# A forward Fourier step on 64x64 tiles of the matrix engine, and a reordered seam between two stages

## The chip, the cores and the metric

The kernel runs on one core of a Trainium2 chip. A core has a matrix engine (TensorE, PE in the profile; its weight loads are listed apart as PEld), a vector engine (VectorE, DVE), a scalar engine (ScalarE, ACT), GpSimd (POOL) and SyncE (SP), whose queue issues most of the transfers. Matmuls write to PSUM, eight banks of 128 partitions by 512 floats. The metric is device microseconds per execution. Before the change three runs took 1424.41, 1427.23 and 1429.85 us, so the median is 1427.23 us.

## The reference, cut to what matters

The input has 4096 positions with 640 columns, and everything is float32.

```
mod = silu(c) @ w_mod                          # six vectors of 640: sa, ca, ga, sb, cb, gb
h = layernorm(x) * (1 + ca) + sa
X = rfft2(h) over positions                    # 4096 real values -> 2049 frequencies
z = X split into 4 blocks of 160 columns       # complex block MLP, two layers, relu,
Y = softshrink(mlp2(relu(mlp1(z))), 0.01)      #   then soft shrink of real and imaginary part
x = x + ga * irfft2(Y)
h = layernorm(x) * (1 + cb) + sb
x = x + gb * ((silu(h @ w_gate) * (h @ w_up)) @ w_down)
```

## The kernel before, in words

The transform of 4096 points is split as 128 by 32. **Stage A** multiplies by a 128-point Fourier matrix and writes its result to memory (`s1`). **Stage B** does the 32-point transforms with their twiddle factors. The frequencies come in eight chunks `ch`, taken in the order `[3, 4, 5, 6, 0, 1, 2, 7]`; a chunk is one tile `g` of 128 partitions by 4 by 640, and a table `tb` with four 128x128 matrices. For each of five column tiles `t` of 128 columns (t = 4 holds the remainders of the four blocks) `stage_b(ch, t)` issues four f32 matmuls, one for each `j`: 128 columns of `g` are the weights, 128 columns of `tb` the moving side. The matrix `tb` couples only partitions with the same `p` (two groups), so half of each 128x128 matrix is zero. An f32 matmul appears in the trace as two weight loads and two matmuls, so one column tile is 8 matmuls there (line L631).

`evac_b` then scales the PSUM bank into `z`, a high part by ScalarE (L638) and a low part by VectorE (L639); for t = 4 it is `rem_high` and `rem_low` (L681, L685), and a round trip through memory. **The block MLP** follows: `stage_l1` (L727, 21 matmuls, PSUM tags p1 and p3), ScalarE and VectorE work on its result (L744 to L769), `stage_l2` (L795, 16 matmuls, tag p2), and the soft shrink on VectorE (`shrink_v`, L819 and L820). **The first inverse step** `stage_i` (L841) has 16 matmuls with 32 rows and 64 columns each, 32 in the trace, whose products go to four banks of the tags p2, p1, p1, p3; ScalarE copies them (L844), and they are written to memory (`s2`).

The whole frequency stage is one hand-written sequence of 32 steps `p = 4 * ch + b`: the layer-1 products of step p, one or two tiles of stage B for the next chunk, then now and then a small matmul `pm` that finishes one of the six vectors (`mod_sum`, L563 and L568), the inverse of an earlier half chunk in even steps, the shrink, and the layer-2 products of step p - 1. Each engine executes its instructions in the order written. Of the eight PSUM banks six belong to tags p1, p2 and p3, two banks each taken in turn; b0 and b1 are single banks: stage B uses b0 (b1 for t = 4), and `pm` uses b0 or b1 where a vector isn't put in p3.

**The seam.** Behind the last step the first four rows of the second half of the kernel are finished without a trip through memory: `first_c`, `first_z` and `first_e` (L1044, L1050, L1057) give them in PSUM as `py`, VectorE and GpSimd add them to `x` and normalise (L1066 to L1105), ScalarE makes the first normalised row (L1119), TensorE transposes rows 0 and 1, then rows 2 and 3 (L1918), and `first_g` takes them through the first gate matrix. In it `high` (L1924) and `whole` (L1932 on ScalarE, L1934 on VectorE) read the transposed rows, and `low` (L1938) makes the low parts for both halves of the rows. The last inverse, `stage_i(7, 1)`, stands behind the products of all four rows. From there on the feed-forward part runs under a planner with its own table of costs; its order is the same in both kernels.

Of the kernel before, what the change touches and what calls it, by code (L numbers as in the profile page):

```python
# [6 lines left out]
F32 = mybir.dt.float32  # L7
F32R = mybir.dt.float32r
# [5 lines left out]
P = 128  # L14
# [7 lines left out]
NCH = 8  # L22
# [4 lines left out]
CE = 4  # L27
LAM = 0.01
# [18 lines left out]
def constants():  # L47
# [38 lines left out]
    tb = tb.transpose(0, 3, 1, 2, 4, 5, 6).reshape(8, 4, 128, 128)[ORDER].reshape(32, 128, 128)  # L86
# [3 lines left out]
    tx = tx.transpose(2, 0, 1, 3).reshape(128, 2)  # L90
# [76 lines left out]
def body(tc, x, w1, b1, w2, b2, wg, wu, wd, c, wm, k_fa, k_tb, k_tx, k_bx, k_ga, k_ge, k_id, out, dbg=None):  # L167
# [4 lines left out]
    def f32(ap):  # L172
        return ap.bitcast(F32)
# [23 lines left out]
    with ExitStack() as top:  # L197
# [3 lines left out]

        def bank0(i, shape, name):
            return ps.tile(shape, F32, tag=f"b{i % 2}", bufs=1, name=name)
# [28 lines left out]
        with ExitStack() as af:  # L232
# [57 lines left out]
            def load_tb(ch):  # L290
                tb = lp.tile([P, 4, 128], F32, tag="tb", bufs=2, name=f"tb{ch}")
                nc.sync.dma_start(tb, k_tb[:, 4 * ch:4 * ch + 4])
                tbs[ch] = tb


            def load_g(ch, lo=0, hi=32, dma=None, cols=(slice(0, D),)):
# [6 lines left out]
                for e in cols:  # L303
                    (dma or nc.sync).dma_start(gs[ch][4 * lo:4 * hi, :, e], src[:, lo:hi, :, e].rearrange("q n j d -> n q j d"))
# [249 lines left out]
            def mod_sum(m, hf=0):  # L554
# [3 lines left out]
                elif m in (2, 5):  # L558
                    if m == 5:
                        gbb.append(low_p.tile([P, 320], F32, tag="m", bufs=4, name=f"gbb{hf}"))  # L560
                    pm = (bank0(1, [P, 512], f"pm{m}_{hf}") if hf else
                          ps.tile([P, 512], F32, tag="p3", name=f"pm{m}_{hf}"))
                    mm(pm[:, :320], ones, acc[:, 320 * hf:320 * hf + 320], start=True, stop=True)  # L563
                    act.activation(gab[:, 320 * hf:320 * hf + 320] if m == 2 else gbb[hf], pm[:, :320], AF.Copy)
                else:
                    pm = bank0(m, [P, 512], f"pm{m}")
# [55 lines left out]

            def stage_b(ch, t):
                g, tb = gs[ch], tbs[ch]
# [9 lines left out]
            def evac_b(ch, t):  # L634
                pb = pbs[ch, t]
                z = lp.tile([P, 2, 2, 258], F32R, tag="z", bufs=4, name=f"z{ch}_{t}")
                zs[ch, t] = z
                act.activation(z[:, 0, :, 0:256], pb, AF.Identity, scale=ca1[:, t:t + 1])  # L638
                dve.scalar_tensor_tensor(z[:, 1, :, 0:256], pb, ca1[:, t:t + 1],  # L639
                                         f32(z[:, 0, :, 0:256]), op0=OP.mult, op1=OP.subtract)  # L640
                if ch == CE:
                    pool.tensor_copy(z[:, 0, :, 0:257:256], f32(edge[:, 0, t]))
# [36 lines left out]
            def rem_high(ch):  # L679
                rt = rts[ch] = low_p.tile([P, 2, 2, 258], F32R, tag="wt", name=f"rt{ch}")  # L680
                act.activation(rt[:, 0, :, 0:256], pbs[ch, 4], AF.Identity, scale=ca1[:, 4:5])  # L681

            def rem_low(ch):
                rt = rts[ch]
                dve.scalar_tensor_tensor(rt[:, 1, :, 0:256], pbs[ch, 4], ca1[:, 4:5], f32(rt[:, 0, :, 0:256]),  # L685
                                         op0=OP.mult, op1=OP.subtract)
# [1902 lines left out]
```

## Time and profile before

| what | value |
|---|---|
| three runs, median | 1427.23 us |
| the profiled execution's own time | 1425.44 us |
| its span | 1423.7 us |
| TensorE busy | 1391.0 us, 98% |
| VectorE, ScalarE, GpSimd busy | 1096.3, 734.0, 536.0 us |
| steps p = 5 to 28 with stage B of chunks 2 to 7 | about 91 to 262 us of the span |
| seam | about 282 to 312 us |

Times in rows are microseconds from the start of the span. A row of the timeline has the start, the time until the last of the merged instructions ended, engine, line, operation, output<-inputs and a count; a square bracket at its end tells for how long the engine was idle before and what ended that. Matmuls are pipelined, so the time to the next matmul's start, not the duration, is what one costs. L12 is line 12 of the kernel that the row belongs to; the changed kernel's lines are about 60 higher (stage B 676, inverse 901, `pm` 580 and 585, `low` 2006).

### The profile page before, as it was taken

The numbers are of one execution on the slowest core, as the hardware profiler recorded it, in microseconds if no ns is written. First come the engines' busy times: TensorE is split into PE (matmuls) and PEld (weight loads), VectorE is DVE, ScalarE is ACT, GpSimd is POOL, SyncE is SP. The second block draws the span as 40 slices with busy tenths as digits, with TensorE's granted clock in tenths as the row PEclk, the third lists the DMA queues.
The fourth block names the chain that finished last, engine by engine and source line by source line (L and its number), as shares of the span: only waits on it lengthen the run. The fifth ranks groups of instructions, "written<-read, shape, count | busy, mean of one in ns | idle before, by whom it ended". The sixth has DMA issues, their size and how long they took to land.

```text
span 1423.7 us, 24436 instructions
## 1 busy us (share of the span) xinstructions
PE 1391.0 (98%) x8840; PEld 1308.9 (92%) x8840; DVE 1096.3 (77%) x1984; ACT 734.0 (52%) x1495; POOL 536.0 (38%) x632
## 2 busy tenths in 40 slices
PE   6899999989999999999999999999999999999999
PEld 2699999968889888999999999999999999999998
DVE  8888898798787888578878777888657668567765
ACT  7855555555444664455555456555444345245432
POOL 5300330135353544224334434433325454145532
PEclk9999999999999999999999999999999999999999
DMA  9866677567668989997877998778886667966552
GB/s 379 318 232 202 213 251 237 192 197 257 243 228 315 326 272 297 347 330 233 292 279 254 356 347 278 237 268 279 310 309 232 215 218 241 358 219 215 206 190 86
DMA packets 183179, 372.17 MB, mean 261 GB/s; under 512 B 21361, under 2 KB 104369, under 8 KB 181393
## 3 DMA queue, kind: packets, MB, share of 16 engines
q1 hardware_dynamic: 175200, 355.12, 72.1%
q0 software_dynamic: 6272, 12.85, 2.9%
q10 hardware_dynamic: 1584, 2.62, 0.5%
q8 instruction: 70, 1.15, 0.3%
q14 instruction: 53, 0.43, 0.1%
HBM read 265.68 MB, written 104.86 MB: 260 GB/s over the span
## 4 chain that ended last, share of the span: by engine, by line
PE 84%; DVE 8%; DMA 4%; ACT 1%; issue 1%; POOL 1%; SPq 0%; DVEq 0%; ACTq 0%; POOLq 0%
PE pd L2458 15%; PE pw L2139 8%; PE pw L2141 8%; PE pw L2140 8%; PE pc L795 5%; PE pd_X L2320 5%; PE pl L727 4%; PE pg L2004 4%; PE pg L2003 4%; PE pg L2005 4%; PE pd_Y L2320 3%; PE pw L2150 2%; PE pw L2152 2%; PE pw L2151 2%; PE pb L631 2%; PE py L1691 2%
## 5 line engine op out<-in xcount | busy, mean ns | idle before, releaser
L2458 PE MATMUL pd<-wdh,a 128*128 128x320 f32 x1040 | 239.1, 310 | 1.1 <-DVE x L2430 1.1
L2458 PEld LDWEIGHTS pd<-wdh,a 128*128 128x128 f32 x1040 | 176.2, 188 | 1.7 <-DVE x L2430 1.4
L2458 PE MATMUL pd<-wdl,a 128*128 128x320 f32 x540 | 166.2, 309 | 0.0
L1446 DVE TENSOR_TENSOR wb<-r,wb 128x512 fp32r<-128x512 f32 (+3 forms) x154 | 151.5, 994 | 12.0 <-ACT wb L1443 9.9
L2139 PE MATMUL pw<-h,wt 128*128 128x384 f32 x416 | 141.2, 340 | 2.2 <-ACT s_x L2158 2.2
L2141 PE MATMUL pw<-h,wt 128*128 128x384 f32 x416 | 140.2, 337 | 0.0
L2140 PE MATMUL pw<-h,wt 128*128 128x384 f32 x416 | 139.9, 336 | 0.0
L2430 DVE TENSOR_TENSOR x<-x,pd 128x320 f32<-128x320 f32 x240 | 109.7, 479 | 39.0 <-PE pd L2458 34.7
L1443 ACT ACTIVATE wb<-r 128x512 fp32r<-128x512 f32 (+3 forms) x170 | 117.4, 704 | 35.2 <-PE pw L2152 25.9
L2139 PE MATMUL pw<-h,wb 128*128 128x384 f32 x312 | 105.0, 336 | 0.9 <-DVE x L2430 0.9
L2140 PE MATMUL pw<-h,wb 128*128 128x384 f32 x312 | 104.6, 335 | 0.0
L2141 PE MATMUL pw<-h,wb 128*128 128x384 f32 x312 | 104.6, 335 | 0.0
L2003 PE MATMUL pg<-ht,wb 128*128 128x512 f32 x260 | 102.3, 393 | 0.0
L2005 PE MATMUL pg<-ht,wb 128*128 128x512 f32 x260 | 101.4, 390 | 0.3 <-DVE wb L1446 0.3
L2458 PEld LDWEIGHTS pd<-wdl,a 128*128 128x128 f32 x540 | 101.4, 188 | 0.3
L2004 PE MATMUL pg<-ht,wb 128*128 128x512 f32 x260 | 101.5, 390 | 0.0
L2158 ACT ACTIVATE s_x<-pw 128x384 f32<-128x384 f32 x52 | 25.4, 489 | 120.3 <-PE pw L2141 119.5
L1674 POOL TENSOR_TENSOR cr<-cr,gab 128x640 f32<-128x640 f32 x28 | 48.0, 1717 | 94.5 <-DMA cr<-s 67.1
L2139 PEld LDWEIGHTS pw<-h,wt 128*128 128x128 f32 x416 | 78.1, 188 | 3.7 <-ACT s_x L2158 3.7
L2140 PEld LDWEIGHTS pw<-h,wt 128*128 128x128 f32 x416 | 78.2, 188 | 0.0
L2141 PEld LDWEIGHTS pw<-h,wt 128*128 128x128 f32 x416 | 78.1, 188 | 0.0
L2294 DVE TENSOR_TENSOR x<-x,pd_X 128x320 f32<-128x320 f32 x144 | 64.5, 484 | 14.2 <-PE pd_X L2320 14.2
(344 smaller groups left out, 3879.8 us busy)
## 6 DMA issues: line engine op xcount, KB each, us to landing
wt<-td SPq DMA_DIRECT2D x104, 512.0 KB, 5.2
hs<-ho SPq DMA_DIRECT2D x52, 512.0 KB, 5.4
h<-hs SPq DMA_DIRECT2D x32, 768.0 KB, 9.0
r<-in_B_w_up_dram SPq DMA_DIRECT2D x36, 640.0 KB, 4.8
r<-in_B_w_gate_dram SPq DMA_DIRECT2D x36, 640.0 KB, 5.1
wdr<-wdd SPq DMA_DIRECT2D x25, 640.0 KB, 5.5
td<-wt SPq DMA_DIRECT2D x25, 512.0 KB, 4.8
g<-s SPq DMA_DIRECT2D x7, 1280.0 KB, 7.3
```

The source lines that it names most:

```text
L795: mm(pc[:M, :W], l, m, start=(i == 0), stop=(i == len(seq) - 1))
L1443: act.activation(wbs[t, n][:, 0, ks, e], raw[t, n][:, ks, e], AF.Copy)
L1446: (pool if onp else dve).tensor_tensor(wbs[t, n][:, 1, ks, e], raw[t, n][:, ks, e], f32(wbs[t, n][:, 0, ks, e]), op=OP.subtract)
L2003: mm(b, wh, hh, start=(kk == 0), stop=False)
L2004: mm(b, wh, hl, start=False, stop=False)
L2005: mm(b, wl, hh, start=False, stop=(kk == 4))
L2139: mm(b, w(0, kp), a[:, kp, 0], start=start and kp == 0, stop=False, skip_group_check=not start)
L2140: mm(b, w(0, kp), a[:, kp, 1], start=False, stop=False, skip_group_check=not start)
L2141: mm(b, w(1, kp), a[:, kp, 0], start=False, stop=kp == 1, skip_group_check=not start)
L2320: mm(bk[b, i][:, :320], x, y, start=new and j == 0, stop=j == len(seq) - 1, skip_group_check=not new)
L2430: dve.tensor_tensor(x2[:, e], x2[:, e], x[0][:, :320], op=OP.add)
L2458: mm(pd[g, hf][0][:, :320], l, m, start=i == 0, stop=i == len(s) - 1 and not (last and len(gs) > 1))
```

## The change

**Stage B from chunk 2 on** (`PK = 2`) uses tiles of 64 rows by 64 columns. The partitions of `g` are reordered on loading so that `p` is the upper or lower half (two transfers of 64 partitions in place of one), and `tb` shrinks to 64 columns without the zero half. A column tile is now 16 f32 matmuls (32 in the trace): for each `j` the two column halves `d` and the two partition halves `p`, each 64x64 weights with 64 moving columns. The two `p` go to different banks. One tile `bt` of two banks holds these for one column tile, or for t = 4 and t = 0 together; it takes the place of b0 and b1 and has no second copy. `z` keeps its size with another order inside, so layer 1 reads its moving side in two pieces; the evacuation of t = 4, and all of chunk 4, takes two instructions where there was one.

**The small matmuls** `pm` that used b0 and b1 take the next bank of p1. **`edges`**, a small product of chunk 4's input, moves from step 12 to step 13.

**The seam.** `stage_i(7, 1)` moves up between the pairs of rows and takes the banks p3, p3, b1, b0. The last of the ten low parts in `first_g` goes to GpSimd.

```diff
-    tx = tx.transpose(2, 0, 1, 3).reshape(128, 2)
+    tx = tx.transpose(0, 2, 1, 3).reshape(128, 2)
...
-                tb = lp.tile([P, 4, 128], F32, tag="tb", bufs=2, name=f"tb{ch}")
-                nc.sync.dma_start(tb, k_tb[:, 4 * ch:4 * ch + 4])
+                n = 128 if ch < PK else 64
+                tb = lp.tile([P, 4, n], F32, tag="tb", bufs=2, name=f"tb{ch}")
+                nc.sync.dma_start(tb, k_tb[:, 4 * ch:4 * ch + 4, 0:n])
...
+                    for p in range(2):
+                        (dma or nc.sync).dma_start(gs[ch][64 * p + 2 * lo:64 * p + 2 * hi, :, e],
+                                                   src[2 * p:2 * p + 2, lo:hi, :, e].rearrange("q n j d -> n q j d"))
...
-                    pm = (bank0(1, [P, 512], f"pm{m}_{hf}") if hf else
-                          ps.tile([P, 512], F32, tag="p3", name=f"pm{m}_{hf}"))
+                    pm = ps.tile([P, 512], F32, tag="p1" if hf else "p3", name=f"pm{m}_{hf}")
...
-                    pm = bank0(m, [P, 512], f"pm{m}")
+                    pm = ps.tile([P, 512], F32, tag="p1", name=f"pm{m}")
...
             def stage_b(ch, t):
+                if ch < PK:
+                    return stage_b0(ch, t)
+                g, tb = gs[ch], tbs[ch]
+                if t not in (0, 4) or (ch, 4 - t) not in bts:
+                    bts[ch, t] = pools["bb"].tile([P, 2, 2, 2, 128], F32, tag="bb", name=f"pb{ch}_{t}")
+                    k = 0
+                else:
+                    k = 1
+                bt = bts[ch, 4 - t if k else t]
+                banks = pbs[ch, t] = [bt[:, p, k] for p in range(2)]
+                pairs[ch, t] = bt[:, :, k].rearrange("c p r k -> c p (r k)")
+                for j in range(4):
+                    for d in range(2):
+                        for p in range(2):
+                            h, q = slice(64 * p, 64 * p + 64), slice(64 * d, 64 * d + 64)
+                            mm(banks[p][q, :, 32 * j:32 * j + 32], g[h, j, 128 * t + 64 * d:128 * t + 64 * d + 64], tb[h, j, :],
+                               start=True, stop=True)
...
-                act.activation(z[:, 0, :, 0:256], pb, AF.Identity, scale=ca1[:, t:t + 1])
-                dve.scalar_tensor_tensor(z[:, 1, :, 0:256], pb, ca1[:, t:t + 1],
-                                         f32(z[:, 0, :, 0:256]), op0=OP.mult, op1=OP.subtract)
+                for o, pb in z_pieces(ch, t, 0):
+                    act.activation(o, pb, AF.Identity, scale=ca1[:, t:t + 1])
+                for (o, pb), (h, _) in zip(z_pieces(ch, t, 1), z_pieces(ch, t, 0)):
+                    dve.scalar_tensor_tensor(o, pb, ca1[:, t:t + 1], f32(h), op0=OP.mult, op1=OP.subtract)
...
-            sums.setdefault(4 * CE - 4, []).append((edges,))
...
+                if p == 4 * CE - 3:
+                    edges()
...
             first_c(1, 0)
+            stage_i(NCH - 1, 1, ("p3", "p3", "b1", "b0"))
             first_c(2, 1)
...
             first_c(3, 0)
-            stage_i(NCH - 1, 1, ("p1", "p1", "p2", "p2"))
...
-                    dve.tensor_tensor(ht0[k][:, 1, c], hx[k][:, c], f32(ht0[k][:, 0, c]), op=OP.subtract)
+                    (pool if h and k == 4 else dve).tensor_tensor(ht0[k][:, 1, c], hx[k][:, c], f32(ht0[k][:, 0, c]), op=OP.subtract)
```

Three places of the order matter later. The first is TensorE in step 29, where `pm` ends the fifth vector sum and the inverse `pi` of half a chunk follows; before:

```order
L568 MATMUL pm_3464<-ones,acc 128x1 [waits DVE_49]
L568 MATMUL pm_3464<-ones,acc 128x1 x4
L841 MATMUL pi_0_0_3475<-tt_0_0_3101,bx 64x320 [waits PE_49]
L841 MATMUL pi_0_1_3476<-tt_0_0_3101,bx 64x320 [waits Activation_49]
L841 MATMUL pi_0_2_3477<-tt_0_0_3101,bx 64x320 [waits Activation_49]
L841 MATMUL pi_0_3_3478<-tt_0_0_3101,bx 64x320
```

and with the change:

```order
L585 MATMUL pm_3855<-ones,acc 128x1 [waits DVE_49,PE_49,Activation_49]
L585 MATMUL pm_3855<-ones,acc 128x1 x4
L901 MATMUL pi_0_0_3866<-tt_0_0_3452,bx 64x320
L901 MATMUL pi_0_1_3867<-tt_0_0_3452,bx 64x320 [waits PE_49,Activation_49]
L901 MATMUL pi_0_2_3868<-tt_0_0_3452,bx 64x320 [waits DVE_49]
L901 MATMUL pi_0_3_3869<-tt_0_0_3452,bx 64x320
```

The third matmul of the inverse takes the p1 bank that `pm` has just filled, so it now waits for VectorE, which reads `pm` into `cb`. The second place is VectorE around that read, with the change (`cl` and `tt` are the shrink's tiles, `u` and `r` the end of layer 1):

```order
L819 SCALAR_TENSOR_TENSOR u_7_1_3842<-pl_1_2_3835,b1r,u_7_1_3841 64x256 [waits Activation_49]
L829 SCALAR_TENSOR_TENSOR r_7_1_3843<-u_7_1_3842,r_7_1_3843 64x256 [waits Activation_49]
L879 TENSOR_SCALAR cl<-tt_0_1_3661 128x640
L880 TENSOR_TENSOR tt_0_1_3661<-tt_0_1_3661,cl 128x640 [waits DVE_49]
L879 TENSOR_SCALAR cl<-tt_1_1_3672 128x640 [waits DVE_49]
L880 TENSOR_TENSOR tt_1_1_3672<-tt_1_1_3672,cl 128x640 [waits DVE_49]
L589 TENSOR_SCALAR cb_76<-pm_3855 128x5 [waits PE_49]
```

This order is that of the kernel before; what is new is that TensorE waits for its last row. The third place is GpSimd in the seam, with the change (`ts` are sums of weights for later tiles, `cr` rows of the inverse, `gt` a table):

```order
L1147 TENSOR_TENSOR ca_74<-ca_74,mhalf 128x1 [waits DVE_49] x2
L2006 TENSOR_TENSOR ht_7_4269<-hx_4_4342,ht_7_4269 128x256 [waits PE_49,Activation_49,Pool_49]
L1558 TENSOR_TENSOR ts_4270<-r_0_4285 128x256 [waits DMAHW7_49,PE_49]
L1558 TENSOR_TENSOR ts_4270<-r_0_4285,ts_4270 128x256 [waits Pool_49]
L1734 DMA gt_4408<-in_k_ga_dram 128x256 [waits DMASW4_49]
L1558 TENSOR_TENSOR ts_4270<-r_0_4285 128x256
L1558 TENSOR_TENSOR ts_4270<-r_0_4285,ts_4270 128x256 [waits Pool_49]
L1742 TENSOR_TENSOR cr_0_4271<-cr_0_4271,gab 128x640 [waits DMAHW1_49]
```

The row of L2006, the moved low part, is new; it stands ahead of the sums and of `cr`, which followed L1147's counterpart (L1079) directly before.

76 lines of the change are left out of this document (57 added, 19 removed).

## The prediction

> **What bounds the kernel now.** I read the page first: its span, the engines' shares and the chain of waits.
>
> ```profile
> span 1423.7 us, 24436 instructions
> PE 1391.0 (98%) x8840; PEld 1308.9 (92%) x8840; DVE 1096.3 (77%) x1984; ACT 734.0 (52%) x1495; POOL 536.0 (38%) x632
> PE 84%; DVE 8%; DMA 4%; ACT 1%; issue 1%; POOL 1%; SPq 0%; DVEq 0%; ACTq 0%; POOLq 0%
> ```
>
> TensorE is the bound, but a share says little about one stage. So I read the stretch with stage B by windows, its TensorE waits, and one stretch where VectorE looks full.
>
> ```profile
> 110.00:262.00 152.00, 151.25 (x1417) 140.87 (x1416) 129.44 (x231) 84.75 (x201) 29.72 (x48) 1.00 0.68 219
> 169.07:191.68 22.61, 22.61 (x226) 20.62 (x224) 22.32 (x35) 12.70 (x30) 8.03 (x11) 1.00 0.68 225
> PE px L863 <- DMA g<-s: 0.3, 1, 0.3
> PE pc L795 <- ACT co L844: 0.3, 1, 0.3
> PE pc L795 <- DVE tt L797: 0.3, 1, 0.3
> ```
>
> The columns are the stretch, its length, and busy time of PE, PEld, DVE, ACT and POOL. From 95 to 285 us TensorE waits only three times, 0.3 us each. So every microsecond taken from its queue shortens the stage, until VectorE (22.32 of 22.61 us in steps 16 to 18) stops it, and every new wait in its queue lengthens it.
>
> **Stage B, the tiles.** What a tile costs now, and what matmuls on part of the array look like, is in the timeline (TensorE, then two rounds of the inverse's weight loads) and in the view of line L841 (minimum, median and maximum ns).
>
> ```profile
> 121.11 1.95 PE L631 MATMUL pb<-tb,g 128*128 128x128 f32 x16
> 122.89 0.95 PE L315 MATMUL pmc<-ones,acc 128*128 128x1 f32 x8
> L841 PE MATMUL pi<-tt,bx x512: 427/427/479, 101.8 to 294.6; 32*64 32x320 f32 x171
> 102.16 0.18 PEld L841 LDWEIGHTS pi<-tt,bx 32*64 32x64 f32 x8
> 102.43 0.18 PEld L841 LDWEIGHTS pi<-tt,bx 32*64 32x64 f32 x8
> 217.19 1.34 PE L841 MATMUL pi<-tt,bx 32*64 32x320 f32 x32
> 218.46 0.70 PE L795 MATMUL pc<-w2a,h 128*128 128x320 f32 x3
> 219.00 0.61 PE L795 MATMUL pc<-w2b,h 128*128 128x320 f32 x3
> 219.44 0.45 PE L795 MATMUL pc<-w2c,r 128*128 128x320 f32 x2
> ```
>
> Two column tiles take 122.89 - 121.11 = 1.78 us, so one takes 0.89 us and a matmul 0.111 us. In the inverse eight tiles start together and a round of 320 columns lasts 102.43 - 102.16 = 0.27 us, 0.84 ns a column. Its first matmuls are 479 - 427 = 52 ns longer than the rest: that is a load of 64 weight columns that nothing covers.
>
> A new tile is 8 rounds of four (32 matmuls, four places of the array). A round needs 64 x 0.84 = 54 ns of stream and 52 ns of weight load; where load and stream overlap, as in the inverse, the longer one and some start cost decide: I take 57 ns, 0.46 us for 8 rounds. The bounds are 54 ns, and 105 ns if load and stream go one after the other.
>
> To this comes the switch. The inverse takes 218.46 - 217.19 = 1.27 us; four rounds are 1.08, the bare load 0.05, so 0.14 us is spread and drain, 0.12 with four tiles in place of eight. The three matmuls behind it take 0.54 us where the next three take 0.44: 0.10 us for bare full-width weights. The way in I put at 0.10 by analogy. Together 0.05 + 0.12 + 0.10 + 0.10 = 0.37 us a visit.
>
> - t = 4 and t = 0 together, six times: 0.91 + 0.37 = 1.28 for 1.78 us, 0.50 less each, 3.0 us.
> - A tile directly ahead of an inverse, ten times: the inverse pays the way in and out anyway, so 0.46 + 0.05 + 0.12 = 0.63 for 0.89 us, 0.26 less, 2.6 us.
> - A tile between full-width matmuls, eight times (six t = 2, and two that a `pm` separates from the inverse): 0.83 for 0.89 us, 0.06 less, 0.5 us.
>
> That is 6.1 us. Whether the array drains between two tilings no row shows: with no drain the ten tiles gain 0.17 more each, 1.7 us. I keep the drain, since it is there between every two shapes the trace has. [...]
>
> Steps 16 to 18 would give 0.26 + 0.50 + 0.26 = 1.0 us of this, but VectorE has 0.29 us to spare there and gets more work (a split pair of 256 columns for one of 512); I count nothing for them, which leaves 5.1 us. Over the whole stretch it has 152.0 - 129.4 = 22.6 us to spare in some 22 steps, and ScalarE more, so the split instructions are hidden; without that cover the gain could fall to 3 us. The second transfer of `g` and SP's issue of it have two steps of about 7 us before their use. Moving `edges` a step later ends its wait for `g`, 0.3 us. The tile without a second copy is read one step earlier than it is refilled, some 6 us; that costs nothing while VectorE lags less.
>
> **The small matmuls.** They come from free banks into p1, whose next banks the inverse takes at once (rows of ScalarE, TensorE and VectorE around steps 14, 24 and 29).
>
> ```profile
> 159.16 0.98 ACT L564 ACTIVATE gbb<-pm 128x320 f32<-128x320 f32 x2 [0.20 <-PE pm L563]
> 159.59 1.38 PE L841 MATMUL pi<-tt,bx 32*64 32x320 f32 x32
> 231.70 1.06 PE L841 MATMUL pi<-tt,bx 32*64 32x320 f32 x24
> 232.18 0.15 DVE L570 COPY sb<-pm 128x5 f32<-128x5 f32 x1
> 265.78 1.33 PE L841 MATMUL pi<-tt,bx 32*64 32x320 f32 x32
> 267.00 0.50 DVE L819 TENSOR_SCALAR cl<-tt 128x640 f32<-128x640 f32 x1
> 268.92 0.83 DVE L820 TENSOR_TENSOR tt<-tt,cl 128x640 f32<-128x640 f32 x1
> 269.67 0.16 DVE L572 TENSOR_SCALAR cb<-pm 128x5 f32<-128x5 f32 x1
> ```
>
> In steps 14, 24 and 29 the inverse's third matmul now waits until `pm` is read, and everything behind it in TensorE's queue waits too. Step 14: the copy ends at 159.16 + 0.98 = 160.14, the inverse starts at 159.59, so 0.55 us. Step 24: 232.33 - 231.70, 0.6 us. Step 29: VectorE reads `pm` only behind two shrinks, and ends at 269.83, where the inverse started at 265.78: 4.05 us. VectorE's part there hangs on the layer-1 products of the same step, so it moves along with TensorE. Nothing behind gives it back: layer 2, the last steps and the seam follow in the same queue. Sum 5.2 us, bounds 4.5 and 5.6.
>
> A wait of 4 us also touches the clock. The windows around the seam show it (last columns: granted clock, DMA).
>
> ```profile
> 294.00:297.30 3.30, 1.01 (x32) 0.36 (x16) 3.12 (x8) 2.23 (x5) 3.14 (x7) 1.00 0.33 111
> 298.20:301.50 3.30, 3.06 (x15) 2.66 (x14) 2.72 (x10) 2.76 (x7) 1.70 (x3) 0.50 0.69 205
> ```
>
> After 2.3 us without a matmul TensorE ran at 0.50 for some 3.4 us. Step 29's wait is longer; half of 3.4 us at most, 1.7, none at least, since part of the slow stretch may fall into the wait itself: I take 1.0 us.
>
> **The seam.** Timeline rows from the last inverse to the first gate product of the planner.
>
> ```profile
> 295.07 0.77 ACT L844 ACTIVATE co<-pi 128x320 f32<-128x320 f32 x2 [6.46 <-PE pi L841]
> 296.36 0.94 ACT L1119 ACTIVATE xn<-x,sa,ca 128x640 f32<-128x640 f32 x1
> 297.35 1.76 PE L1918 MATMUL pt<-idn,xn 128*128 128x128 f32 x10 [2.34 <-ACT xn L1119]
> 301.25 1.02 DVE L2497 TENSOR_SCALAR xn<-x,b1m,ca 128x640 f32<-128x640 f32 x1 [0.44 <-POOL ca L1079]
> 302.00 0.87 POOL L1490 TENSOR_TENSOR ts<-r,ts 128x256 f32<-128x256 f32 x1
> 302.19 5.35 DVE L1938 TENSOR_TENSOR ht<-hx,ht 128x256 fp32r<-128x256 f32 x5
> 305.31 1.61 POOL L1674 TENSOR_TENSOR cr<-cr,gab 128x640 f32<-128x640 f32 x1 [0.45 <-DMA cr<-s]
> 306.02 1.49 ACT L1932 ACTIVATE hx<-pt,sb,cb 128x256 f32<-128x256 f32 x3
> 308.03 0.42 DVE L1938 TENSOR_TENSOR ht<-hx,ht 128x256 fp32r<-128x256 f32 x1
> 308.51 0.73 PE L1965 MATMUL pg<-ht,wh 128*128 128x512 f32 x2 [1.50 <-DVE ht L1938]
> 310.30 1.55 DVE L1446 TENSOR_TENSOR wb<-r,wb 128x512 fp32r<-128x512 f32 x2
> 311.39 0.39 PE L2003 MATMUL pg<-ht,wb 128*128 128x512 f32 x1
> ```
>
> With the inverse earlier its copies no longer stand ahead of row 0 on ScalarE, so the transposes come sooner by at most the 2.34 us that TensorE waited for that row. That alone is worth little: rows 2 and 3 end at 302.27 by VectorE's own chain, and five low parts follow there that last 5.35 us, where one undisturbed takes 0.42 (308.03), because GpSimd's sums and `cr` hold them up; only then come the low parts that TensorE waits for. But the moved low part stands ahead of these sums in GpSimd's queue, and waits for ScalarE's `hx`. So the sums come later, the five may run from 302.3 to 304.4, and the products would start when TensorE is free: at 308.51 - 1.50 = 307.0 as now, and up to a microsecond sooner without the slow clock; in all up to some 3 us less. The sums then meet VectorE's next work, the low parts of `wb` (1.55 us) that TensorE needs within 2 us of its first planned product. If they hold it up as now, nothing is left. I take 1.8 us less, bounds 3.0 less and 0.3 more (the late products of rows 2 and 3).
>
> **Sum.** 5.1 + 0.3 + 1.8 less, 5.2 + 1.0 more: 1.0 us less than the profiled execution's 1425.4, 1424.4 us. That execution lies 1.8 us below the median of 1427.2; between the two bases I say **1425 us**. A difference under 0.5%, 7 us, I call no change, as the three runs alone spread over 5 us.
>
> **The rivals.**
> - The waits on p1 don't bind, because VectorE reaches `cb` in time. Then 6.1 + 0.3 + 1.8 are left: 1417 us. For it speaks only that VectorE isn't full in step 29; against it that the order of its rows is fixed.
> - Load and stream of a 64x64 tile do not overlap, 105 ns a round: 8 x 48 ns x 30 tiles is 11.5 us more, stage B loses 5.4 us, and the sum is 1425.4 + 5.4 + 6.2 - 2.1 = 1435 us, slower. It decides from 82 ns a round on, where the 6.1 us are gone. Against it: the inverse's rounds go at the stream's pace. For it: no row has rounds this short.
> - The queue doesn't bring 32 or 64 such matmuls as fast as that. The fastest run in the trace is the inverse's 32 in 1.27 us, 40 ns each. At this pace a pair takes 2.54 us (0.76 more), a lone tile 1.27 (0.38 more), tile and inverse 2.54 for 2.16 (0.4 more): 4.6 + 3.0 + 4.0 = 11.6 us more, 1441 us. The inverse, though, has larger products and is bound by them. [...]
>
> **Chances.** 0.68 for the forecast, with its own range from 1418 (8.5 us from stage B, 3.0 from the seam, 4.5 lost) to 1430 (3 us from stage B, nothing from the seam, 5.6 and 1.7 lost); 0.17, 0.10 and 0.05 for the rivals in their order. With the spread of the runs the range is 1417 to 1432. Below 1420 lies most of the first rival and a little of the forecast, 0.20; above 1434 the third, half of the second and a little more, 0.13; in between 0.67.
>
> **What would show it.** The line of stage B: 64x64 rows, pairs at 1.28 us and rounds at 57 ns. In step 29 a wait of TensorE of about 4 us for VectorE's `cb`, half clock behind it, and two of 0.6 us. In the seam, five undisturbed low parts and products from 306 us of the old scale. No wait in step 29, or rounds over 80 ns, would make the prediction wrong.

## The result and the profile after

The change made the kernel slower. Seven runs gave a median of 1434.56 us (1432.23 to 1437.23), seven of the kernel before 1426.31 us: the ratio is 1.0055, with a 95% interval from 1.0041 to 1.0069. I had put 0.67 on no difference beyond 0.5% and 0.13 on slower; the time lies above my range. The profiled execution took 1434.7 us, and its page differs from the one before like this (span, busy shares, chain of waits):

```profile
span 1432.9 us, 25963 instructions
PE 1391.5 (97%) x9560; PEld 1301.1 (91%) x9560; DVE 1093.8 (76%) x1993; ACT 735.0 (51%) x1505; POOL 535.1 (37%) x633
PE 65%; DVE 7%; DMA 3%; ACT 2%; issue 1%; POOL 1%; SPq 0%; DVEq 0%; ACTq 0%; POOLq 0%
```

TensorE's busy time is what it was (1391.5 us for 1391.0), and the span is 9.2 us longer. The equal busy time is a balance: in steps 5 to 28 it falls by 3.9 us (170.15 to 166.28), and in step 29 it grows by 3.6 (7.34 to 10.95), at a granted clock of 0.50 for most of it. So the answer lies in what TensorE waits for, and in that clock. These are its longest waits between 90 and 285 us, where the kernel before has three of 0.3 us (line, releaser, us in total, times, longest):

```profile
PE pi L901 <- DVE cb L589: 3.4, 1, 3.4
PE pi L901 <- DVE tt L857: 1.7, 2, 0.9
PE pm L580 <- DVE acc L568: 1.6, 1, 1.6
PE pc L855 <- DVE tt L857: 1.1, 1, 1.1
```

The first row is step 29, which I had expected; the others are in steps 5, 6, 14 and 18, in or behind the new pairs of tiles, and I had not.

**Where the time went.** A step begins with its first layer-1 product (L727 before, L787 after). From these starts come the lengths below; the last two rows end at the last matmul, and "first planned product" is the first of the planner's gate products (L2003, L2071).

| stretch | before, us | after, us | difference |
|---|---|---|---|
| start to step 5 | 90.95 | 91.08 | +0.13 |
| steps 5 to 28 | 171.21 | 171.85 | +0.64 |
| step 29 | 7.34 | 14.30 | +6.96 |
| step 30 | 6.76 | 6.74 | -0.02 |
| step 31 to the first planned product | 35.13 | 31.56 | -3.57 |
| the next 20 planned products | 15.14 | 17.15 | +2.01 |
| the rest | 1093.61 | 1096.60 | +2.99 |

**The tiles themselves did as forecast.** Two rows of the timeline of the change, a pair and a lone tile:

```profile
93.73 1.16 PE L676 MATMUL pb<-tb,g 64*64 64x64 f32 x64
101.21 0.69 PE L676 MATMUL pb<-tb,g 64*64 64x64 f32 x32
```

The pair takes 0.47 us longer (0.466 from first to last start) for eight more rounds, 58 ns a round. Where nothing else changed, the steps are shorter by what I had counted: step 7 by 0.07 us (lone tile), steps 8 and 10 by 0.28 and 0.26 (ahead of the inverse), steps 9 and 17 by 0.51 (pair).

**A wait that the pair brings.** The view of the tile `rt`, the high half of the remainder (t = 4), which ScalarE takes out of PSUM; the kernel before has no such wait:

```profile
L739 ACT ACTIVATE rt<-pb,ca x12: 467/472/477, 98.6 to 242.3; 128x256 fp32r<-128x256 f32 x12
its engine sat idle before it (us, times) until:
  DVE z L696: 8.4, 6
```

Six pairs, and six times ScalarE waits until VectorE has read the *other* tile, t = 0. No data goes from that read to this one. The two tiles lie in two halves of the same two banks, and this instruction now has a wait for VectorE in the program that runs. No run here lets the two reads overlap; only the ordering wait is seen. What follows from it stands in the timeline of steps 5 and 6 (rows of ScalarE, VectorE and TensorE in order of time; rows that the reading does not need are left out between them):

```profile
95.05 0.69 ACT L694 ACTIVATE z<-pb,ca 128x512 fp32r<-128x512 f32 x1
97.82 0.73 DVE L696 SCALAR_TENSOR_TENSOR z<-pb,ca,z 128x512 fp32r<-128x512 f32 x1
98.48 0.52 PE L787 MATMUL pl<-z,w1a 128*128 128x256 f32 x3
98.59 0.84 ACT L739 ACTIVATE rt<-pb,ca 128x256 fp32r<-128x256 f32 x2 [2.85 <-DVE z L696]
99.31 0.41 ACT L828 ACTIVATE r<-u 64x256 fp32r<-64x256 f32 x1
99.75 0.42 DVE L829 SCALAR_TENSOR_TENSOR r<-u,r 64x256 fp32r<-64x256 f32 x1 [1.20 <-ACT r L828]
...
102.24 0.88 DVE L857 TENSOR_TENSOR tt<-pc,b2t 128x320 f32<-128x320 f32 x2
102.78 1.34 PE L901 MATMUL pi<-tt,bx 32*64 32x320 f32 x32 [0.87 <-DVE tt L857]
...
107.08 0.52 PE L787 MATMUL pl<-z,w1a 128*128 128x256 f32 x3
```

ScalarE is done with `z` at 95.7 and stands still until 98.59, because VectorE's read for its half of `z` ends only at 98.55. The next activation on ScalarE, `r`, is late with it; VectorE waits 1.20 us for that; all of VectorE's queue is late; and 3 us further on TensorE waits 0.87 us for it. Step 6 takes 107.08 - 98.48 = 8.60 us, before 7.30.

**Step 29.** TensorE's inverse in the timeline, VectorE's rows that it waits for, and the windows around it (stretch, length, busy PE, PEld, DVE, ACT, POOL, granted clock, DMA):

```profile
266.54 0.75 PE L901 MATMUL pi<-tt,bx 32*64 32x320 f32 x4
269.70 0.83 DVE L880 TENSOR_TENSOR tt<-tt,cl 128x640 f32<-128x640 f32 x1
270.44 0.16 DVE L589 TENSOR_SCALAR cb<-pm 128x5 f32<-128x5 f32 x1
270.65 2.43 PE L901 MATMUL pi<-tt,bx 32*64 32x320 f32 x28 [3.35 <-DVE cb L589]
```

```profile
266.90:270.10 3.20, 0.40 (x4) 0.00 (x0) 2.64 (x5) 0.41 (x1) 0.00 (x0) 1.00 0.59 131
270.20:276.90 6.70, 6.25 (x42) 4.75 (x43) 0.89 (x3) 1.43 (x4) 0.00 (x0) 0.50 0.65 250
277.00:283.90 6.90, 6.90 (x72) 5.83 (x71) 2.71 (x6) 3.90 (x10) 1.31 (x3) 1.00 0.06 22
```

The wait is there, for the instruction that I had named, and then TensorE runs at half clock for 6.8 us, twice as long as the stretch at the seam before the change (3.4 us).

**The seam.** GpSimd, VectorE, ScalarE and TensorE in the timeline of the change, and behind them one row of VectorE from the kernel before:

```profile
309.50 1.76 DVE L2006 TENSOR_TENSOR ht<-hx,ht 128x256 fp32r<-128x256 f32 x5
312.38 1.49 ACT L2000 ACTIVATE hx<-pt,sb,cb 128x256 f32<-128x256 f32 x3
314.01 0.74 POOL L2006 TENSOR_TENSOR ht<-hx,ht 128x256 fp32r<-128x256 f32 x1 [5.07 <-issue]
314.70 1.19 POOL L1558 TENSOR_TENSOR ts<-r 128x256 f32<-128x256 f32 x1
317.55 3.99 DVE L1689 TENSOR_TENSOR wdl<-wdr,wdh 128x640 fp32r<-128x640 f32 x1
317.89 0.75 POOL L1558 TENSOR_TENSOR ts<-r 128x256 f32<-128x256 f32 x1
319.28 1.57 POOL L1742 TENSOR_TENSOR cr<-cr,gab 128x640 f32<-128x640 f32 x1
328.13 0.50 PE L2073 MATMUL pg<-ht,wb 128*128 128x512 f32 x1 [0.41 <-DVE wb L1514]
330.96 0.50 PE L2073 MATMUL pg<-ht,wb 128*128 128x512 f32 x1 [1.18 <-DVE wb L1514]
```

```profile
313.40 0.82 DVE L1621 TENSOR_TENSOR wdl<-wdr,wdh 128x640 fp32r<-128x640 f32 x1 [0.20 <-ACT wdh L1617]
```

The moved low part stands 5.07 us at the head of GpSimd's queue (the row names no releaser; the low part needs ScalarE's last `hx`, which ends at 313.87), the sums wait behind it, and VectorE's five low parts take 1.76 us where they took 5.35. This is the gain. The sums then come more than 9 us later against TensorE's first planned product, and meet VectorE's low part of w_down, which takes 3.99 us; the kernel before has 0.82 there. VectorE has no pause from there to 331 us, and TensorE waits 0.41 and 1.18 us for `wb`, whose low parts come late in that queue (before, 0.34 us in all). So VectorE's rows were longer where GpSimd's ran beside them, 5.35 us for 1.76 and 3.99 for 0.82. By what they were held up these rows do not show, nor that the earlier start counts: the 3.99 us begin 0.34 us ahead of GpSimd's sum (317.55 and 317.89).

### The profile page after: what moved, and what is told of

Same layout as the page of the kernel before. It is cut to its first block, busy times and chain, and to the rows that moved or that the text cites. A ratio compares the mean times of both kernels' runs of the same rounds, so it can differ in the third digit from the quotient of the medians.

```text
span 1432.9 us, 25963 instructions
## 1 busy us (share of the span) xinstructions
PE 1391.5 (97%) x9560; PEld 1301.1 (91%) x9560; DVE 1093.8 (76%) x1993; ACT 735.0 (51%) x1505; POOL 535.1 (37%) x633
## 4 chain that ended last, share of the span: by engine, by line
PE 65%; DVE 7%; DMA 3%; ACT 2%; issue 1%; POOL 1%; SPq 0%; DVEq 0%; ACTq 0%; POOLq 0%
PE pd L2526 14%; PE pw L2207 8%; PE pw L2209 8%; PE pw L2208 8%; PE pd_X L2388 5%; PE pd_Y L2388 3%; PE pg L2072 3%; PE pg L2071 3%; PE pg L2073 3%; PE pw L2218 2%; PE pw L2220 2%; PE pw L2219 2%; DVE wb L1514 2%; PE py L1759 1%; PE pd_Z L2388 1%
## 5 line engine op out<-in xcount | busy, mean ns | idle before, releaser
L2071 PE MATMUL pg<-ht,wb 128*128 128x512 f32 x260 | 102.3, 393 | 0.0
```

The lines of the kernel that those rows point to most:

```text
L2071: mm(b, wh, hh, start=(kk == 0), stop=False)
```

## The experiments

Each was timed beside the kernel before, whose median lay between 1426.3 and 1428.5 us from one group to the next, so ratios to it are compared.

| kernel | median, us | ratio to before | 95% interval |
|---|---|---|---|
| the change | 1434.56 | 1.0055 | 1.0041 to 1.0069 |
| remainder's copy first | 1431.62 | 1.0019 | 1.0007 to 1.0030 |
| `pm` of step 29 in b0 | 1428.90 | 1.0009 | 0.9997 to 1.0020 |
| both ("repaired") | 1423.45 | 0.9965 | 0.9953 to 0.9978 |
| the change without the seam | 1435.24 | 1.0046 | 1.0031 to 1.0061 |
| repaired, low part on VectorE | 1425.37 | 0.9988 | 0.9976 to 1.0000 |
| repaired, inverse behind | 1425.41 | 0.9990 | 0.9978 to 1.0002 |
| repaired, no seam | 1424.61 | 0.9985 | 0.9974 to 0.9997 |
| repaired, no tiles | 1425.53 | 0.9988 | 0.9975 to 1.0001 |
| repaired, again | 1424.69 | 0.9978 | 0.9963 to 0.9992 |
| repaired, no seam, again | 1425.30 | 0.9980 | 0.9968 to 0.9992 |
| repaired, `pm` of step 24 in p3 | 1423.64 | 0.9969 | 0.9958 to 0.9980 |
| repaired, another low part | 1425.19 | 0.9980 | 0.9967 to 0.9993 |

Below the change, the first four kernels were timed as one group on one chip, the next four as a second on another, the last four as a third. The repaired kernel, which is in two groups, shows how far a ratio moves between them: 0.9965 and 0.9978.

### The remainder's copy first

```diff
                 for q in todo:
                     stage_b(*q)
+                    if q[1] == 0:
+                        rem_high(q[0])
                     if q[1] < 4:
                         evac_b(*q)
...
-                if b == 1 and ch + 1 < NCH:
-                    rem_high(ch + 1)
                 on(tail_l1, p)
```

> The changed kernel, with ScalarE's copy of the remainder tile (rem_high) put ahead of the evacuation of the t = 0 tile instead of behind it; all work is the same. In the trace of the change ScalarE sat idle 8.4 us in six places ahead of `rt` until VectorE had read the other tile of the pair (`z` low part), which lies in the same two banks; the kernel before has none of this. Theory 1 (the shared banks): this late ScalarE is what makes VectorE late in the steps behind each pair, where TensorE now waits (0.87 us in step 6, 1.60 in 14, 0.87 and 0.20 in 18, about half a microsecond in 24 and 26). Without it ScalarE has no such wait and some 4 to 5 us come back: 1430 us. Theory 2 (more work): VectorE is late because it does the remainder's low part in two instructions of 256 columns, and more in steps 13 to 16; then the order makes no difference: 1434 to 1435 us, with the same waits.

The ratio fell from 1.0055 to 1.0019, 0.36% or 5.1 us (by the two intervals some 2.6 either way), so theory 1 holds and theory 2 falls: the same instructions in another order. The view of `rt` (ScalarE) in this kernel, and TensorE's longest waits from 100 to 285 us:

```profile
L739 ACT ACTIVATE rt<-pb,ca x12: 467/473/477, 96.1 to 239.7; 128x256 fp32r<-128x256 f32 x12
its engine sat idle before it (us, times) until:
  PE pb L676: 2.6, 4
```

```profile
PE pi L901 <- DVE cb L589: 3.4, 1, 3.4
PE pm L580 <- DVE acc L568: 1.2, 1, 1.2
PE pi L901 <- DVE tt L857: 0.9, 1, 0.9
```

ScalarE no longer waits for VectorE there. Step 6 is back to 7.41 us (8.60), step 18 falls from 9.60 to 8.36, step 26 from 7.69 to 7.24; the 1.60 us in step 14 fall only to 1.2, so that wait has a second cause. Step 22, with 0.9 us of wait, is longer than in the change (8.46 for 7.65); what such a step can meet is told with the repeated runs below.

### The small matmul of step 29 in b0

```diff
-                    pm = ps.tile([P, 512], F32, tag="p1", name=f"pm{m}")
+                    pm = bank0(m, [P, 512], f"pm{m}") if m == 4 else ps.tile([P, 512], F32, tag="p1", name=f"pm{m}")
```

> The changed kernel, with the small matmul result `pm` of step 29 alone back in bank b0, which is free there, so that the inverse behind it finds both p1 banks. Theory 1 (wait and clock): the inverse's wait for VectorE's `cb` (3.4 us) goes, and with it the half clock, which lasted 6.8 us from 270.1 on and cost about half of the 6.3 us that lie behind the wait, 3.1 us; step 29 comes back to 7.3 us: 6.5 to 7 us less, 1428 us, and no clock below full speed after 250 us. Theory 2 (the wait alone): the slow clock is not tied to it and comes again at the seam: 3.4 to 4 us less, 1431 us. Theory 3 (the time is only moved): VectorE is what bounds steps 29 to 31, and TensorE waits for it a little later: 1433 us or more.

The ratio fell to 1.0009, by 0.46% or 6.6 us: theory 1. The windows of steps 28 and 29 in this kernel:

```profile
262.80:269.90 7.10, 7.10 (x80) 6.41 (x79) 5.39 (x11) 3.90 (x10) 1.22 (x3) 1.00 0.71 231
270.00:277.30 7.30, 7.30 (x75) 6.23 (x74) 3.91 (x9) 3.90 (x10) 1.36 (x3) 1.00 0.70 270
```

TensorE is busy all the time at full clock, and step 29 takes 7.32 us for 14.30. Of these 6.98 us the wait was 3.35; 6.3 us of the half clock lay behind it, half of that is 3.1 us, and 0.5 us stays unassigned. The edit takes wait and half clock away together, so the 3.1 us are worked out and not measured apart. A half clock did come later in this trace, at 338 us behind another wait of 2.9 us (matmuls of 0.47 us for 0.31).

### Both edits together

> Both edits together: the remainder's copy first, and `pm` of step 29 in its own bank. If each does what theory 1 says and the two do not touch, the gains add: 4.5 and 6.7 us from 1434.6, so 1423 to 1424 us, 2 to 3 us below the kernel before; stage B then shows what my prediction counted for the tiles (steps 5 to 28 some 4 us shorter than before). If VectorE is the bound of these steps, a part is lost: 1426 us or more.

The gains add and a little more: the ratio is 0.9965, 0.90% under the change, and below the kernel before as well. Within this group the remainder's copy brings 5.5 us (1428.90 to 1423.45) and `pm` 8.2 (1431.62 to 1423.45), where the steps of the traces account for 3.8 and 7.0; the rest is no more than a ratio moves between groups. Steps 5 to 28 did not become 4 us shorter than before in its trace but 0.6 (170.57 for 171.21), with steps 6 and 22 at 8.4 us each. In the traces where these two steps run undisturbed (7.4 and 7.2), the stretch takes 168.05 us, 3.2 under the kernel before.

### The change without the seam

```diff
-            stage_i(NCH - 1, 1, ("p3", "p3", "b1", "b0"))
             first_c(2, 1)
...
             first_c(3, 0)
+            stage_i(NCH - 1, 1, ("p1", "p1", "p2", "p2"))
...
-                    (pool if h and k == 4 else dve).tensor_tensor(ht0[k][:, 1, c], hx[k][:, c], f32(ht0[k][:, 0, c]), op=OP.subtract)
+                    dve.tensor_tensor(ht0[k][:, 1, c], hx[k][:, c], f32(ht0[k][:, 0, c]), op=OP.subtract)
```

> The changed kernel with the seam as before: the last inverse behind all first rows, in banks p1 and p2, and the last low part on VectorE. From the traces: up to the first planned gate product the seam gave back 3.6 us of the 7.7 lost by then, and in the ten microseconds behind it 2.0 us were lost again, since GpSimd's sums, now behind the moved low part, hold up VectorE's low parts (one took 3.99 us, where the kernel before shows 0.82). If the seam is worth the difference: 1.6 us more, 1436 us, with a half clock at the seam again. If the half clock after step 29 is what took the place of the seam's (the seam has none because the clock has only just come back), the seam is worth nothing or less: 1433 to 1435 us.

The ratio is 1.0046 against 1.0055: no difference that this measurement can tell, and not the 1.6 us more. In its trace the stretch from step 31 to the first planned product is 35.27 us again (31.56 with the seam), the first 20 planned products take 15.25 us (17.15), and what is left 1094.4 (1096.6). Both halves of my reading show, and they cancel. The reason that I gave for the second theory, the clock, is not borne out: this trace has half clock at step 29 (271.35 to 278.18 us) and at the seam again (308.90 to 312.31), and its mean granted clock is 0.993, where the change has 0.996.

### The two parts of the seam on the repaired kernel

The edits are those of the last diff on the repaired kernel: its last pair of lines alone (low part back on VectorE), its two lines on `stage_i` alone (inverse behind), and all of it.

> The repaired kernel (remainder's copy first, `pm` of step 29 in b0) with the last low part of the rows 2 and 3 back on VectorE; the inverse stays between the pairs of first rows. Theory 1 (GpSimd's queue): what the seam brings and what it takes both come from the moved low part, which waits 5 us at the head of GpSimd's queue and keeps the sums behind it away from VectorE's five low parts (1.76 us for 5.35), and sends them later into VectorE's low part of w_down (3.99 us for 0.82). Then this kernel loses the gain: from the start of step 31 to the first planned gate product 34 to 35.5 us where the repaired kernel has 31.57, and wins the loss back: no waits of TensorE for `wb` and `chl` of over 0.5 us in the first 20 planned products. In all the same time within 1.5 us. Theory 2 (the inverse's place): the earlier inverse lets the transposes start earlier, and that is the gain: 31.6 to 32.5 us here as well, and 2 us less in all.

> The repaired kernel with the last inverse back behind all first rows (banks p1 and p2), the low part still on GpSimd. Theory 1: the stretch to the first planned product stays near 31.6, at most 33 us (the half clock comes back behind an idle stretch of 2.3 us and costs up to 1 us), and the loss behind it stays too: 0 to 1.5 us more in all than the repaired kernel. Theory 2: 34 to 35 us, 3 us more in all.

> The repaired kernel without both parts of the seam. On the kernel of the change this made no measurable difference (1.0046 against 1.0055 of the kernel before). If the seam's gain of 3.6 us is given back in the feed-forward part (2.0 us right behind it, 0.7 to 1.2 us near 504 us, which only kernels with the seam show so far), the same again: within 1.5 us of the repaired kernel, 1423 us. If the seam is worth what my prediction gave it, 1.8 us: 1425 us.

| kernel | step 31 to first planned product | next 20 products | rest |
|---|---|---|---|
| repaired (both parts) | 31.57 | 17.15 | 1095.40 |
| low part on VectorE | 36.87 | 15.34 | 1095.46 |
| inverse behind | 32.86 | 17.15 | 1096.62 |
| neither | 35.29 | 14.84 | 1093.84 |

Theory 1 holds for both: the gain and its loss go with the low part on GpSimd, and beside it the inverse's place is worth 1.3 us. (The 36.87 us, over the 34 to 35.5 of theory 1, hold a half clock behind a wait of 2.6 us: a matmul of 0.63 us for 0.39 at 311.65 us.) Without the moved low part the five low parts take 5.47 us again, and w_down's 0.82 (timeline of the first of the three kernels, VectorE and GpSimd):

```profile
300.71 5.47 DVE L2006 TENSOR_TENSOR ht<-hx,ht 128x256 fp32r<-128x256 f32 x5
300.52 0.86 POOL L1558 TENSOR_TENSOR ts<-r,ts 128x256 f32<-128x256 f32 x1
313.50 0.82 DVE L1689 TENSOR_TENSOR wdl<-wdr,wdh 128x640 fp32r<-128x640 f32 x1 [0.20 <-ACT wdh L1685]
```

The times of these three (0.9985 to 0.9990) all lay 2 to 2.5 per mille above the repaired kernel's, timed in another group, which left open whether the seam brings 3 us on the repaired kernel after all.

### The tiles alone

```diff
-PK = 2
+PK = 8
```

(and with it the layouts, split instructions and banks of stage B as before.)

> The repaired kernel with the 128x128 tiles for all chunks (PK = 8: layouts, split instructions and shared banks as before the change); the seam and the places of `pm` (p1 in steps 14, 19 and 24, b0 in step 29) as changed. It gives the price of the tiles alone. By my sum, 5.1 us more than the repaired kernel: 1428 to 1429 us, the steps with one tile 0.06 to 0.28 and the steps with a pair 0.5 us longer. If VectorE sets the pace of most steps, the tiles bring less: under 2.5 us more, 1425 to 1426 us. If the tiles' waits that are left (VectorE's results for the inverse in steps 6, 18 and 22) come from the tiles, they are gone here.

The ratio is 0.9988; beside the repaired kernel's 0.9965 and 0.9978 that is 1.4 to 3.3 us for the tiles. The steps say more: 5 to 28 take 171.82 us here, and 168.05 with tiles where steps 6 and 22 are undisturbed, so the tiles are worth 3.77 us. Lone tiles and pairs are longer here by what I had said (step 8 by 0.28, step 9 by 0.51 us). But step 14 is *shorter* without tiles, 9.04 us for 10.01, and step 5 the same, 7.42: in both TensorE waits for VectorE in the tiled kernels (1.2 us for `acc`, 1.1 us for `tt`), and in step 5 that takes the whole gain of its pair. Of the steps behind a pair 6, 18 and 26 gain nothing either, 7.40, 8.36 and 7.24 us with tiles for 7.30, 8.04 and 7.19. In step 18 the inverse is drawn out from 1.33 to 1.90 us by a wait for VectorE's `tt`, whose last instruction ends at 185.92 us (repaired kernel without the seam, whose steps 6 and 22 are undisturbed); in step 6 TensorE waits 0.22 us for ScalarE's copies `co`, and ScalarE had waited 1.22 us for VectorE's `u`. So VectorE sets the pace there, directly or by way of ScalarE; for step 26 no wait is long enough to show it. Of the prediction's 5.1 us about 1.3 are lost.

This kernel also prices the rest of the stage: against the kernel before, steps 12 and 13 together are 0.46 us shorter (`edges`), step 14 is 0.39 and step 24 0.69 us longer (`pm` on p1).

### Repeated beside each other, and two small edits

The repaired kernel and the same without the seam, unchanged:

> The repaired kernel a second time, beside the same kernel without the seam on one chip, since the two were timed in different calls and their ratios (0.9965 and 0.9985) leave open whether the seam brings 3 us there or nothing. If the seam is worth what the traces add up to (3.7 us earlier to the first planned gate product, 3.7 to 4 us longer from there to the end): within 1 us of the kernel without it. If it brings the difference of those ratios: 2.5 to 3 us below it.

> The repaired kernel without both parts of the seam, on the same chip as the run before it: equal within 1 us if gain and loss of the seam cancel, 2.5 to 3 us slower if they do not.

0.9978 and 0.9980 on one chip: the seam is worth nothing that can be measured, to within about 2 us. The two traces differ by 1.2 us: with the seam the first planned product comes 3.70 us earlier, and 2.36 and 0.12 us are lost behind it.

The traces also show why steps 6 and 22 differ from execution to execution. GpSimd and VectorE ahead of step 22, in step 21 of the repaired kernel (the second trace of it):

```profile
206.98 3.36 POOL L609 TENSOR_TENSOR wdf<-wdf,gbb 128x640 f32<-128x640 f32 x2 [0.45 <-DMA wdf<-in_B_w_down_dram]
207.15 3.48 DVE L806 TENSOR_TENSOR h<-h,h 128x256 fp32r<-128x256 f32 x2
```

VectorE's two low parts of `h`, 0.42 us each when alone, take 3.48 us beside GpSimd's scaling of w_down, whose start hangs on a transfer. In the change that work starts at 211.69, when the second of the low parts, which begin at 210.78 and 211.38, is almost done, and step 22 takes 7.65 us. In the kernel before the same work of GpSimd (207.25 us, 4.58 us long) meets `acc`, which takes 5.12 us for 0.88, and from 160.37 us on `r`, which takes 1.73 us for 0.42. Ahead of step 6 VectorE waits for a transfer of `wm`, 0.89 us in the first trace of the repaired kernel. In the five repaired traces whose first steps ran about 1.5 us faster, two of them without any half clock (mean granted clock 1.000), step 22 was 0.9 to 1.2 us longer, and in four of them step 6 by 0.7 to 1.0: part of what is won there is given back.

```diff
-                    pm = bank0(m, [P, 512], f"pm{m}") if m == 4 else ps.tile([P, 512], F32, tag="p1", name=f"pm{m}")
+                    pm = bank0(m, [P, 512], f"pm{m}") if m == 4 else ps.tile([P, 512], F32, tag="p3", name=f"pm{m}")
```

> The repaired kernel with the small matmul result `pm` of step 24 in p3 in place of p1. In step 24 the inverse's 32 matmuls take 1.94 us, elsewhere 1.33, and the rest is the wait for VectorE's copy of `pm`. Theory 1 (the wait for the bank): it goes, as p3's other bank has been read by then, and step 24 falls from 8.71 to about 8.1 us, 0.6 us less in all (too little for the times to tell, the step shows it). Theory 2: the wait only moves to VectorE's read of the layer-1 sum `u` in p3, and step 24 stays over 8.5 us.

Theory 1: step 24 falls from 8.71 to 8.11 us, the inverse's row from 1.94 us (first fence, the repaired kernel) to 1.33 (second, this one).

```profile
229.62 1.94 PE L901 MATMUL pi<-tt,bx 32*64 32x320 f32 x32
```

```profile
229.09 1.33 PE L901 MATMUL pi<-tt,bx 32*64 32x320 f32 x32
```

With 1423.64 us and 0.9969 (0.9958 to 0.9980) it is the fastest version of its group, though not told apart from the repaired kernel.

```diff
-                    (pool if h and k == 4 else dve).tensor_tensor(ht0[k][:, 1, c], hx[k][:, c], f32(ht0[k][:, 0, c]), op=OP.subtract)
+                    (pool if h and k == 0 else dve).tensor_tensor(ht0[k][:, 1, c], hx[k][:, c], f32(ht0[k][:, 0, c]), op=OP.subtract)
```

> The repaired kernel with the first of the five low parts of rows 2 and 3 on GpSimd in place of the last (k = 0 for k = 4). Its input `hx` comes from VectorE some 2.3 us before the last one. Theory 1 (the head of GpSimd's queue decides): GpSimd's sums start 2 to 2.5 us sooner, and VectorE's low part of w_down behind them is held up less (below 2.5 us, 3.99 with the last low part), so the first 20 planned products take 15.5 to 16.5 us instead of 17.15, while the stretch from step 31 to the first of them stays at 31.6 or grows by less than a microsecond because the sums now meet the low parts left on VectorE: 0.5 to 1 us less in all. Theory 2 (the sums meet something of VectorE's wherever they start): what is gained behind is lost ahead, no change.

Theory 2, and more strongly than its wording: the stretch to the first planned product grows to 34.72 us, the next 20 products fall to 14.53, and the time stays. GpSimd waits 2.86 us in place of 5.07, and the sums now meet the last three of VectorE's low parts:

```profile
300.26 0.74 POOL L2006 TENSOR_TENSOR ht<-hx,ht 128x256 fp32r<-128x256 f32 x1 [2.86 <-DVE hx L2002]
301.46 5.08 DVE L2006 TENSOR_TENSOR ht<-hx,ht 128x256 fp32r<-128x256 f32 x3 [0.18 <-ACT hx L2000]
309.17 0.83 DVE L1689 TENSOR_TENSOR wdl<-wdr,wdh 128x640 fp32r<-128x640 f32 x1 [0.20 <-ACT wdh L1685]
```

## Why the prediction was wrong

By its own steps, against the two profiled executions and the runs that price each step (us, minus is less time):

| step of the prediction | predicted | measured | from |
|---|---|---|---|
| tiles of stage B | -5.1 | -3.8 | 171.82 to 168.05, without and with tiles |
| "costs nothing" in the buffers of stage B | 0 | +3.8 | 168.05 to 171.85, repaired and changed |
| `edges` a step later | -0.3 | -0.5 | steps 12 and 13 without tiles |
| `pm` on p1, steps 14 and 24 | +1.15 | +1.1 | 0.39 and 0.69 |
| `pm` on p1, step 29, and the clock | +5.05 | +6.96 | 14.30 against 7.34 |
| seam | -1.8 | +1.4 | -3.57, +2.01 and +2.99 behind it |
| start | 0 | +0.1 | |
| sum | -1.0 | +9.1 | the spans 1423.7 and 1432.9 differ by 9.2 |

**Right.** The price of a round (57 ns forecast, 58 measured), of the three kinds of visit (0.50, 0.26 and 0.06 us), the waits on p1 in steps 14 and 24, and the place, cause and releaser of the wait in step 29. The sizes of the visits were counted with a drain between two tilings, which was an estimate that no row shows by itself; the steps directly ahead of an inverse gained 0.26 to 0.28 us, where that count gives 0.26 and one without a drain 0.43. The kernel before takes 0.09 us over the pace of its rows from a tile of L631 into the inverse (100.86 + 8 x 0.111 = 101.75, the inverse starts at 101.84) and 0.14 us behind it; what fills this time no row shows. The rivals are out: no round took 105 ns, the queue brought 32 matmuls in 0.47 us where the third rival needed 1.27, and the p1 waits bind.

**The step that failed** is the one on stage B's buffers. I looked only for when the new tile without a second copy is refilled, found 6 us, and wrote that this costs nothing. I did not ask who reads the two halves of its banks, and in which order. In the program the t = 0 tile is evacuated by ScalarE and VectorE first, the remainder by ScalarE after that; with one bank for both, ScalarE waits for VectorE in every pair, 8.4 us in all, and 3.8 us of that arrive at TensorE. The experiment with the remainder first shows this directly; it needs no other instruction and no other bank.

**Mis-sized.** The half clock behind step 29: I allowed 1.7 us at most, half of one slow stretch of 3.4 us. It lasted two such stretches, 6.8 us, nearly all behind the wait, and cost about 3.1; the wait itself was 3.35 us for 4.05 forecast. The tiles: I let VectorE take 1.0 us of their gain, in steps 16 to 18, and called the split instructions hidden elsewhere, because it had 22.6 us to spare over the stage. The spare time was an average. Steps 5, 6 and 14, behind or in a pair, had none, and step 26 gained nothing either; the fallback of 3 us that I named for lost cover was nearer than the 5.1.

**The seam's mechanism was right and its sum was not.** The moved low part did shield the five low parts (5.35 to 1.76 us), and the sums met VectorE's next work. I valued the first at up to 3 us, it was 3.6, and took 1.8 as a middle. I had written that nothing is left if they are held up as now; that was the outcome. What was held up first was the low part of w_down and not, as I named it, that of `wb`; TensorE then did wait for `wb`, 1.6 us, behind it in VectorE's queue. The 2.99 us of the rest are not all the seam's. Traces of six other kernels with the low part moved have a rest of 1094.6 to 1096.6 us, and a seventh 1099.7 with a half clock; five kernels that leave it or move another have 1093.8 to 1095.9. Their means differ by 0.7 us, by 0.7 as well where neither has a half clock in the rest, and by 1.3 where both have one, so about 1 us of it goes with the seam, and the +1.4 of the table is that of two single executions; the times with and without the seam do not differ. Most of the 2.99 us are TensorE's waits for VectorE's low part `chl` (L1749; 2.7 us, before 0.4). The other changed kernels wait 0.2 to 1.3 us for it, with the low part moved or not; why this one trace has twice as much stays open.

## What to carry to other kernels

When two results are packed into one PSUM bank, list every reader of that bank by engine in program order: here readers of unrelated halves waited for one another (8.4 us in six pairs), and putting one engine's reads together ahead of the other's took that wait away at no price. Spare time of an engine counts only in the step where it is needed; a step whose waiting engine is the tight one gains nothing from a faster neighbour (step 5, 7.42 us with and without the new tiles). Moving an operation to GpSimd also moves what stands behind it in its queue, so price the place where that work will then meet VectorE (here 3.99 us for 0.82).

## What the runs showed of the hardware that was not expected

**The half clock came in pieces of 3.41 us, one or two, and the length of the wait alone does not decide it.** In the two traces before and with the change the granted clock is 0.50 from 72.78 to 76.19 and from 298.06 to 301.47 us (before), and from 72.16 to 75.57 and from 270.13 to 276.96 us (change): three times 3.41 us and once 6.83. The wait of 3.35 us in step 29 goes with the 6.83, that of 2.34 at the seam before with 3.41; in the change two waits of 1.20 and 0.47 us, at 69.74 and 71.36 us, go with 3.41, and one of 1.60 us in step 14 and one of 1.93 at 679.40 us with none. Behind the wait of 2.59 us in the repaired kernel with the low part on VectorE a matmul still took 0.63 us for 0.39 when 4.50 us had passed, longer than one piece. The wait of 2.7 us in the kernel with another low part had none: its mean granted clock of 0.999 leaves room for one piece, and that one shows at 670 us, in matmuls of 0.47 us for 0.31.

**The changes of the clock lay whole steps of 3.413 us apart, and equal waits did not cost the same.** In the change the clock changed at 72.16, 75.57, 270.13 and 276.96 us, the last three 1, 58 and 60 steps behind the first; before at 72.78, 76.19, 298.06 and 301.47 us, 1, 66 and 67 steps. One wait of 1.93 us for ScalarE's `s_z` is cut by an edge of these steps in both traces, into 1.51 and 0.42 us before (from 672.01 us) and 0.33 and 1.60 in the change (from 679.40), and the clock stays at 1.00. Behind the same wait (1.93 to 1.94 us) the matmuls come to take 0.47 us for 0.31 in the kernels with the inverse behind and with another low part, and stay at 0.31 in the second trace of the repaired kernel. In the step ahead of a slow piece TensorE stood idle for 1.80 and 2.34 us before, for 1.67 and 2.83 in the change. Within the first slow piece it stood idle for 0.52 us at step 29, where a second followed, and for 0.24 us at the seam before and not at all near 74 us, where none did. So the same wait cost a piece in one kernel and none in another. Idle time within one step is not the whole rule: 1.82 us of it before, from 29.52 us, were followed by a clock of 1.00; what else counts, no run tells.
